# Linear attention ahead of an expert layer: query features projected a second time, transposed, with the exponent's shift added by one-hot products

## The chip, the core and the metric

One core of one Trainium2 chip. TensorE (PE, with its weight loads PEld), VectorE (DVE), ScalarE (ACT), GpSimd (POOL) and the DMA queue that SyncE issues (SP). The metric is the device time of one execution in microseconds; less is better.

## What is computed

Attention with random features (4 batches, 8 heads, 576 positions, head size 64, 128 features), and then a dense mixture of 8 experts on the 2304 tokens of 512 that it gives. In the reference's words:

```python
def phi(x):
    proj = np.einsum('bhsd,md->bhsm', x, omega)
    sq = np.sum(x * x, axis=-1, keepdims=True) / 2.0
    h = proj - sq
    h = h - np.max(h, axis=-1, keepdims=True)
    return np.exp(h) / np.sqrt(m)
q_p, k_p = (phi(q_s), phi(k_s))
kv = np.einsum('bhsm,bhsd->bhmd', k_p, v)
z = np.sum(k_p, axis=2)
num = np.einsum('bhsm,bhmd->bhsd', q_p, kv)
den = np.einsum('bhsm,bhm->bhs', q_p, z)[..., None] + 1e-06
...
for e in range(E):
    h = np.maximum(x @ w1[e], 0.0)
    ye = h @ w2[e]
    out += P[:, e:e + 1] * ye
```

`x` is num / den. `P` comes from gate logits `x @ w_gate` by eight rounds of row and column scaling. All is fp32.

## The kernel before, in words

**Attention.** The work is cut into 36 jobs, 18 for keys and 18 for queries; a job is 128 rows of eight heads (four tiles of 128 by 128, two heads in each). `jobs` lists them: five key jobs, then key and query jobs in turn, then six query jobs alone. `tick` (L847) writes the program of one step: projections, maxima and shifts of the job now, transposes of the next, feature transposes of a query job one step old, numerators and quotients of one two steps old. In the trace's names: `tp` are transposes of raw rows (L374), copied to `th` (L377, L379); `pp` are projections (L389), 8 matmuls, in two row groups of 64; DVE takes maxima (L399), sums the shift (L404) and adds it to one half (L406), ACT takes exps, the other half's with the shift as bias (L415, L419). For keys the features are multiplied by the values (`kv`, L426). For queries they are transposed on TensorE (`qp`, L485), copied by ACT to `qt` (L492), and multiplied by the keys' sums (`np`, L509); DVE divides (L524 to L528), and the tokens are transposed again (`xp`, L544) and copied to `xf` (L550). All matmuls of this stage share six PSUM banks in turn. `squares` (L343) is done by ACT, and its sum by five halvings on POOL (L353).

**Between.** Tokens stand in three chunks of 768. `token_operands` (L101) makes of a chunk seven operands, each cast to a high part on ACT (L119, L123) with the low part beside it, and stores them to DRAM; the sums among them are on POOL, for the last chunk on DVE (L115). `first_splits` and `split` do the same for weights (L272, L276, L246, L247).

**Experts.** Each matrix product is taken as a 2 by 2 of blocks with seven products in place of eight (`ORDER`, L91), and each of these as three matmuls of high and low parts (`first`, L623: `hx`, `hz`; `second`, L737: `x`, `z`, `w`). The first unit starts with the last chunk, whose operands are not reloaded: their matmuls follow their casts.

**What sets the order.** The attention's instructions are pinned: each engine runs them in the order in which `tick` writes them, by dependencies that a loop adds behind `tick`'s calls. After that a scheduler orders the instructions. Loads are issued on SP in the order in which the program names them.

```python
    jobs += k_of(0) + [kr(0)]
    jobs += mix(k_of(1), q_of(0))
    jobs += mix(k_of(2) + [kr(1)], q_of(1))
    jobs += mix(k_of(3), q_of(2))
    jobs += q_of(3) + [qr(0), qr(1)]
```

Of the kernel before, what the change touches and what calls it, by code (L numbers as in the profile page):

```python
# [9 lines left out]
F32 = mybir.dt.float32  # L10
# [12 lines left out]
def moe_attention_kernel(  # L23
# [51 lines left out]
    ps_cm = tc.tile_pool(name="ps", bufs=6, space=bass.MemoryType.PSUM)  # L75
# [4 lines left out]
    def bank(name):  # L80
        return ps[0].tile([P, 512], F32, tag="b", name=name)
# [11 lines left out]
    pinned = []  # L93

# [6 lines left out]
    def token_operands(c, x):  # L101
# [6 lines left out]
        gate_steps = logits(c, x)  # L108
        if last:
            next(gate_steps)  # L110
# [11 lines left out]
        def low(i, o, t):  # L122
            nc.vector.tensor_tensor(t[:, 1], o, raw(t[:, 0]), op=ALU.subtract)  # L123
            xdram[c, i] = xd.tile([P, 2, 2, HL], F32, name=f"xd{c}_{i}")
            nc.sync.dma_start(out=xdram[c, i], in_=raw(t))

        if last:
            for i in ORDER:
                n = len(traced)
# [5 lines left out]
                pinned.extend(traced[n:])  # L135
                xop[0, c, i] = t
                first(0, c, i, 0)
                first(0, c, i, 1)
# [5 lines left out]
        if c == 0:  # L144
            at = {i: {3: q(1, 1), 7: q(0, 1), 2: q(1, 0)}.get(i, q(0, 0)) for i in ORDER}
            plan = "|c1 |c3 l1.s5|c2 l3|c5 l2.s7| l5.s6|c7 |c6 l7| l6.s4| |c4 | l4|"
        else:
            at = {1: q(0, 0), 3: q(1, 1), 2: q(1, 0)}
            for n, i in enumerate((5, 6, 7, 4)):
                at[i] = vts[n].rearrange("p h c -> p (h c)")[:, : 2 * HL].rearrange("p (k t) -> p k t", k=2)  # L150
            plan = "|s5.c1.c3 s7.l1|c2 l3.s6|c5 l2.s4|c7 l5|c6 l7|c4 l6.l4|"
        tiles = {}
        for n, step in enumerate(plan.split()):
            for part in step.split("|"):
                for what in part.split(".") if part else ():
# [3 lines left out]
                    elif what[0] == "c":  # L159
                        tiles[i] = cast(i, at[i])  # L160
                    else:
                        low(i, at[i], tiles.pop(i))
                yield
            next(gate_steps, None)


    def logits(c, x):
# [4 lines left out]
        for h in range(2):  # L172
            lp = bank("lp")
# [8 lines left out]
        yield  # L182
        for h, lg in enumerate(lgs):
            gp = bank("gp")
# [24 lines left out]

    def split(u, w, i):  # L210
# [8 lines left out]
        if w == 1:  # L219
# [10 lines left out]
            o = {1: q(0, 0), 7: q(0, 1), 2: q(1, 0), 4: q(1, 1)}[i] if i not in (5, 6, 3) else tmp[u]  # L230
        else:
# [15 lines left out]
        (nc.vector if u > 0 or (w == 2 and i in (1, 6, 7, 4)) else nc.gpsimd).tensor_tensor(lo, o, raw(hi), op=ALU.subtract)  # L247
# [3 lines left out]
    def first_splits():  # L251
# [10 lines left out]
        for step in "|s5.c1 | l1|c2 |c5 l2| l5.s6.s7| |c4 |c6 l4|c7 l6.s3| l7| |c3 | l3|".split():  # L262
            for part in step.split("|"):
                for what in part.split(".") if part else ():
# [9 lines left out]
                    else:  # L274
                        hi, lo = wt[0, 1, i]
                        nc.vector.tensor_tensor(lo, at[i], raw(hi), op=ALU.subtract)  # L276
                yield


    sc_cm = tc.tile_pool(name="sc", bufs=1, reuse_waits="tile")  # L280
# [9 lines left out]
    om_ps = bank("om_ps")  # L290
    nc.tensor.transpose(om_ps[:, :P], oms.rearrange("p a d -> p (a d)"), ident)
    omt = sc.tile([P, M], F32, name="omt")
    nc.scalar.copy(omt, om_ps[:, :M])

# [16 lines left out]
    def load(which, key):  # L311
# [3 lines left out]
        if key[0] == "r":  # L315
# [5 lines left out]
            else:  # L321
                t = rw.tile([P, H, 1, D], F32, tag=f"{which}r", bufs=2 if which == "q" else 1, name=f"{which}r")
# [11 lines left out]
        else:  # L334
            t = rw.tile([P, H, 2, D], F32, tag=which, bufs=4, name=which)
# [7 lines left out]
    def squares(which, key):  # L343
# [10 lines left out]
        nc.gpsimd.tensor_tensor(o[..., :1], s[..., :1], s[..., 1:2], op=ALU.add)  # L354
        nc.gpsimd.tensor_scalar_mul(o[..., 2], o[..., 0], -1.0)
        sqt[which, key] = o

# [9 lines left out]
    def transposes(jb):  # L367

        which, key, hh = jb[:3]
        tin = rawt[which, key].rearrange("p h j d -> p (h j d)")  # L370
        tp = bank("tp")
        for i in range(4):
            o = (4 * hh + i) * P
            nc.tensor.transpose(tp[:, i * P : (i + 1) * P], tin[:, o : o + P], ident)  # L374
        th = sc.tile([P, 4, P], F32, tag="th", bufs=2, name="th")
        if which == "k":
# [632 lines left out]
```

## Time and profile before

| | us |
|---|---|
| median of 3 runs (lowest to highest) | 1613.35 (1613.24 to 1614.67) |
| profiled execution, its own time | 1611.28 |
| span of its profile | 1609.4 |
| PE busy in the span | 1574.7 |
| DVE busy | 1388.4 |
| ACT busy | 774.8 |
| POOL busy | 298.1 |

The span runs from the first instruction of the profiled execution to its last; the execution's own time is 1.9 longer and is what is compared. Busy times are per engine and overlap. Matmuls are pipelined: a row's printed time holds the last one's way through the array, and what a group takes from the engine is read from its start to the start of the next.

### The profile page before, as it was taken

What the parts mean: (1) busy time and instruction counts of PE and PEld (TensorE: products, weight loads), DVE (VectorE), ACT (ScalarE), POOL (GpSimd) and SP (SyncE); (2) the same over time, 40 slices, a digit from 0 to 9 for tenths busy, and PEclk for the clock granted to TensorE, in tenths of its full rate; (3) what the DMA queues carried; (4) which work ended last, traced back from release to release, by engine and by line L of the source; (5) the groups of instructions that cost most, each with busy time, mean ns of one, the idle gap of its engine ahead of it and who ended that gap; (6) DMA issues with size and microseconds to landing.
All of it is one profiled execution on the core that took longest, in us unless ns stands there. A gap on an engine that the chain in (4) does not pass through costs nothing.

```text
span 1609.4 us, 31434 instructions
## 1 busy us (share of the span) xinstructions
PE 1574.7 (98%) x12318; PEld 1543.1 (96%) x12318; DVE 1388.4 (86%) x2721; ACT 774.8 (48%) x1396; POOL 298.1 (19%) x304
## 2 busy tenths in 40 slices
PE   7998899999999999999999999999999999999998
PEld 6877899999999999999999999999999999999997
DVE  5998798999888987989898988889898889889777
ACT  7987565444344444434354444444443444444333
POOL 6664321101021111101021111112010111110003
PEclk9999999999999999999999999999999999999999
DMA  8646865666665665656656665746565566655552
GB/s 205 153 146 240 305 229 203 212 209 208 220 217 192 233 211 171 224 197 215 206 206 213 211 220 181 253 170 223 203 208 210 211 216 212 212 189 198 193 197 79
DMA packets 105314, 329.79 MB, mean 205 GB/s; under 512 B 14800, under 2 KB 43984, under 8 KB 105168
## 3 DMA queue, kind: packets, MB, share of 16 engines
q1 hardware_dynamic: 105168, 327.79, 60.2%
q8 instruction: 98, 1.61, 0.4%
q14 instruction: 48, 0.39, 0.1%
HBM read 306.53 MB, written 21.23 MB: 204 GB/s over the span
## 4 chain that ended last, share of the span: by engine, by line
PE 86%; DVE 10%; ACT 2%; POOL 1%; issue 1%; DMA 0%; SPq 0%; DVEq 0%; ACTq 0%
PE hx L650 24%; PE x L751 23%; PE hz L650 18%; PE z L751 12%; PE w L751 6%; DVE sm L687 2%; DVE out L777 2%; PE pp L389 1%; DVE bl L687 1%; DVE sqs L399 1%; DVE wl L247 1%; POOL sq L353 1%; DVE sl L726 1%; PE tp L374 1%; DVE xs L123 1%
## 5 line engine op out<-in xcount | busy, mean ns | idle before, releaser
L650 PE MATMUL hx<-xs,wh 128*128 128x384 f32 x1536 | 372.2, 336 | 2.7 <-ACT out L767 1.2
L777 DVE SCALAR_TENSOR_TENSOR out<-x,prob,out 128x256 f32<-128x256 f32 x497 | 234.2, 477 | 59.5 <-PE x L751 57.8
L650 PE MATMUL hz<-xs,wh 128*128 128x384 f32 x1152 | 281.7, 337 | 0.0
L650 PEld LDWEIGHTS hx<-xs,wh 128*128 128x128 f32 x1536 | 268.6, 188 | 4.3 <-ACT xs L119 2.0
L216 POOL TENSOR_TENSOR st<-st 128x512 f32<-128x512 f32 x79 | 126.3, 1598 | 702.6 <-DVE wl L247 698.1
L650 PEld LDWEIGHTS hz<-xs,wh 128*128 128x128 f32 x1152 | 203.2, 189 | 0.7 <-ACT xs L119 0.4
L650 PE MATMUL hx<-xs,wl 128*128 128x384 f32 x768 | 198.7, 335 | 0.0
L729 ACT ACTIVATE bh<-hr 128x512 fp32r<-128x512 f32 x144 | 91.2, 633 | 211.6 <-PE x L751 206.9
L777 DVE SCALAR_TENSOR_TENSOR out<-z,prob,out 128x256 f32<-128x256 f32 x252 | 120.3, 478 | 56.5 <-PE z L751 55.9
L725 ACT CAST sh<-sm 128x512 fp32r<-128x512 f32 x144 | 89.6, 622 | 152.7 <-PE z L751 106.1
L246 ACT CAST wh<-st 128x512 fp32r<-128x512 f32 x172 | 102.9, 620 | 104.6 <-PE hx L650 43.9
L650 PE MATMUL hz<-xs,wl 128*128 128x384 f32 x576 | 151.7, 336 | 0.0
L687 DVE SCALAR_TENSOR_TENSOR sm<-hr,sm 128x256 f32<-128x256 f32 x288 | 137.1, 476 | 2.6
L650 PEld LDWEIGHTS hx<-xs,wl 128*128 128x128 f32 x768 | 138.4, 188 | 0.0
L247 DVE TENSOR_TENSOR wl<-st,wh 128x512 fp32r<-128x512 f32 x169 | 121.8, 730 | 12.0 <-ACT wh L246 11.5
L687 DVE SCALAR_TENSOR_TENSOR bl<-hr,bh 128x512 fp32r<-128x512 f32 x144 | 119.5, 830 | 0.1
L751 PE MATMUL x<-wh,sh 128*128 128x256 f32 x576 | 116.9, 283 | 2.6 <-DVE out L777 1.6
L751 PE MATMUL x<-wl,sh 128*128 128x256 f32 x576 | 118.2, 282 | 0.7 <-DVE wl L247 0.7
L751 PE MATMUL x<-wh,sl 128*128 128x256 f32 x576 | 117.2, 282 | 0.0
L751 PE MATMUL z<-wl,sh 128*128 128x256 f32 x576 | 117.2, 281 | 0.0
L751 PE MATMUL z<-wh,sl 128*128 128x256 f32 x576 | 115.3, 282 | 1.7 <-DVE sl L709 1.7
L751 PE MATMUL z<-wh,sh 128*128 128x256 f32 x576 | 116.6, 281 | 0.2 <-DVE out L777 0.2
(161 smaller groups left out, 3410.5 us busy)
## 6 DMA issues: line engine op xcount, KB each, us to landing
xs<-xd SPq DMA_DIRECT2D x329, 768.0 KB, 4.4
st<-in_moe_w_dram SPq DMA_DIRECT2D x64, 512.0 KB, 5.1
xd<-xs SPq DMA_DIRECT2D x21, 768.0 KB, 4.3
k<-in_k_dram SPq DMA_DIRECT2D x8, 512.0 KB, 7.1
v<-in_v_dram SPq DMA_DIRECT2D x8, 512.0 KB, 6.5
q<-in_q_dram SPq DMA_DIRECT2D x8, 512.0 KB, 7.5
out_dram<-out SPq DMA_DIRECT2D x32, 128.0 KB, 1.9
kr<-in_k_dram SPq DMA_DIRECT2D x4, 128.0 KB, 6.6
```

The costliest lines, as they stand in the source:

```text
L123: nc.vector.tensor_tensor(t[:, 1], o, raw(t[:, 0]), op=ALU.subtract)
L216: nc.gpsimd.tensor_tensor(o, a, b, op=op)
L246: nc.scalar.copy(hi, o)
L247: (nc.vector if u > 0 or (w == 2 and i in (1, 6, 7, 4)) else nc.gpsimd).tensor_tensor(lo, o, raw(hi), op=ALU.subtract)
L353: nc.gpsimd.tensor_tensor(s[..., :w], s[..., :w], s[..., w : 2 * w], op=ALU.add)
L374: nc.tensor.transpose(tp[:, i * P : (i + 1) * P], tin[:, o : o + P], ident)
L650: nc.tensor.matmul(pb, lhsT=a[:, k, g * P : (g + 1) * P], rhs=x[:, b, k, :], start=i in (1, 5, 2) and j == 0, stop=j == len(prods) - 1, sk ...
L687: nc.vector.scalar_tensor_tensor(o, in0=a, scalar=0.0, in1=b, op0=ALU.max, op1=op)
L725: nc.scalar.copy(sh, sm)
L729: nc.scalar.activation(bh, a[:, 1:], AF.Relu)
L751: nc.tensor.matmul(pb, lhsT=ops[s][i][a][:, f], rhs=wt[u, 2, i][b][:, f], start=bool(start) and j == 0, stop=j == len(prods) - 1, skip_gro ...
L777: nc.vector.scalar_tensor_tensor(o, in0=pb, scalar=p, in1=o, op0=ALU.mult, op1=ALU.add)
```

## The change

What it does, part by part:

- **Query features.** The projection of a query job is kept for the maxima alone. Its shift (three numbers of a row summed, twice, into a small tile `cx`) is turned by two matmuls against the identity (`turned_shifts`, `cp`), cast by ACT to a high part and reduced by DVE to a low part beside it (`shift_copy`, `ct`). `features` projects a second time with the operands exchanged, 512 columns a matmul, so that features come out transposed, and adds the shift by eight one-hot products (`pick`, fp32r) into the same banks. ACT takes two exps of 512 columns from PSUM to `qt`. Transposes, copies, bias exps and the add of the old way are gone for queries.
- **Half transposes.** `turn` transposes 64 rows at a time, into two banks; raw rows of a key and a query job share two banks and are copied by ACT.
- **Banks and order.** Six banks are now three pairs, `bk`, `bt`, `bq`; `period` takes the place of `tick` and writes a key and a query job together. One query job (`qr(0)`) moves into the paired part, so 13 pairs and five query jobs alone remain. Tokens are numbered in the order in which the query jobs give them.
- **Squares.** POOL adds twice (the first key job's and the last query job's not at all), and DVE reduces the rest.
- **Token and weight parts.** Low parts of chunks 0 and 1 and of the first unit's first weights move from DVE to POOL. The first unit's second weights have their sums made by POOL during the attention's end, and all their low parts on DVE.
- **First unit.** Its chunks are taken as 1, 2, 0. Chunk 1's operands are used where they are cast; `first` of chunk 1 and of four of seven operands of chunk 2 are left to the scheduler, ahead of the second products.

```diff
-    def bank(name):
-        return ps[0].tile([P, 512], F32, tag="b", name=name)
+    def bank(name, tag=None):
...
+        return ps[0].tile([P, 512], F32, tag=tag, name=name)
...
-            nc.vector.tensor_tensor(t[:, 1], o, raw(t[:, 0]), op=ALU.subtract)
+            (nc.vector if last else nc.gpsimd).tensor_tensor(t[:, 1], o, raw(t[:, 0]), op=ALU.subtract)
...
-        w = D
-        while w > 2:
-            w //= 2
-            nc.gpsimd.tensor_tensor(s[..., :w], s[..., :w], s[..., w : 2 * w], op=ALU.add)
...
+            for w in (D // 2, D // 4) if n < D else ():
+                nc.gpsimd.tensor_tensor(s[..., :w], s[..., :w], s[..., w : 2 * w], op=ALU.add)
...
+            nc.vector.tensor_reduce(o[..., 0], s[..., :n], axis=AX.X, op=ALU.add)
...
+    def turn(tiles, name, tag):
+
+        banks = [bank(name, tag) for _ in range(2)]
+        for i, a in enumerate(tiles):
+            for h in range(2):
+                r = slice(h * 64, (h + 1) * 64)
+                nc.tensor.transpose(banks[h][:, i * 64 : (i + 1) * 64], a[r], ident[r, r])
+        return [bk[:, : 64 * len(tiles)] for bk in banks]
...
+    def turned_shifts(jb):
+
+        cx = cxq.pop(jb)
+        cp = bank("cp", "bt")[:, :P]
+        for g in range(2):
+            nc.tensor.matmul(cp[g * 64 : (g + 1) * 64], lhsT=cx[:, g], rhs=ident, start=True, stop=True)
+        cps[jb] = cp
...
+    def features(jb):
+
+        th, ct = ths.pop(jb), cts.pop(jb)
+        fp = [bank("fp", "bt") for _ in range(2)]
+        for g in range(2):
+            r = slice(g * D, (g + 1) * D)
+            nc.tensor.matmul(
+                fp[g], lhsT=omt[r], rhs=th[r].rearrange("p i s -> p (i s)"), start=True, stop=False,
+                skip_group_check=True,
+            )
+        for i in range(4):
+            for g in range(2):
+                r = slice(g * D, (g + 1) * D)
+                nc.tensor.matmul(
+                    fp[g][:, i * P : (i + 1) * P], lhsT=pick[r, i], rhs=ct[r], start=False, stop=i == 3,
+                    skip_group_check=True,
+                )
+        fps[jb] = fp
+
+    def query_exps(jb):
+
+        qts[jb] = [sc.tile([P, 4, P], F32, tag="ex", bufs=6, name="qt") for _ in range(2)]
+        for t, fp in zip(qts[jb], fps.pop(jb)):
+            nc.scalar.activation(t.rearrange("p i s -> p (i s)"), fp, AF.Exp)
...
-        return [NCH - 1] + list(range(NCH - 1)) if u == 0 else list(range(NCH))
+        return list(range(1, NCH)) + [0] if u == 0 else list(range(NCH))
...
+    pairs = list(zip(k_of(0) + [kr(0)], none))
+    pairs += zip(k_of(1), q_of(0))
+    pairs += zip(k_of(2) + [kr(1)], q_of(1) + [qr(0)])
+    pairs += zip(k_of(3), q_of(2))
+    pairs += [(None, jb) for jb in q_of(3) + [qr(1)]]
```

How PE's order moves in the paired part, one key and one query job before (all names as above):

```order
L389 MATMUL pp<-omt,th 128x128 x8
L374 MATMUL tp<-ident,q 128x128 x4
L485 MATMUL qp<-ident,ex 128x128 x8
L389 MATMUL pp<-omt,th 128x128 x8
L374 MATMUL tp<-ident,k 128x128 x4
L509 MATMUL np<-kvs,qt 64x65 x16
L426 MATMUL kv<-v_96,ex 64x65 x16
```

And now (`fp` is the transposed projection at L500 and the one-hot products at L507, `cp` the turned shift):

```order
L457 MATMUL pp<-omt,th 128x128 x8
L432 MATMUL xp<-ident,xt 128x64 x8
L500 MATMUL fp<-th,omt 128x512 x2
L507 MATMUL fp<-ct,pick 128x128 x8
L457 MATMUL pp<-omt,th 128x128 x8
L432 MATMUL tp<-ident,k 128x64 x8
L432 MATMUL tp<-ident,q 128x64 x8
L612 MATMUL np<-kvs,qt 64x65 x16
L546 MATMUL kv<-v_107,ex 64x65 x16
L482 MATMUL cp<-ident,cx_103 64x128 x2
```

The transposes of both raw jobs stand together, all between the key projections and the numerators uses 64 rows of the array, and `qp` is gone.

ACT in the same place, before:

```order
L492 COPY qt<-qp 128x512 x2
L419 ACTIVATE ex<-pp,cn 128x128 x4
L415 ACTIVATE ex<-ex 128x512
L349 ACTIVATE sq<-q 128x1024
L377 COPY th<-tp 128x512
L419 ACTIVATE ex<-pp,cn 128x128 x4
L272 CAST wh<-st 128x512
L415 ACTIVATE ex<-ex 128x512
```

And now (`ct` is the cast of the shift, `qt<-fp` the query's exps):

```order
L489 CAST ct<-cp 128x128
L309 CAST wh<-t 128x512
L656 COPY xf<-xp 128x4x64 x2
L517 ACTIVATE qt<-fp 128x512 x2
L539 ACTIVATE ex<-pp,cn 128x128 x4
L535 ACTIVATE ex<-ex 128x512
L979 COPY th<-tp 128x8x64 x2
L398 ACTIVATE sq<-qr 128x512
```

The query's exps come first, behind a cast of weights and the token copies, then the key's, and the copies of raw transposes behind both.

PE at the attention's end, before (`lp`, `gp` belong to the gate, `hx` is the first expert matmul):

```order
L485 MATMUL qp<-ident,ex 128x128 x8
L509 MATMUL np<-kvs,qt 64x65 x16
L485 MATMUL qp<-ident,ex 128x128 x8
L544 MATMUL xp<-ident,xt 128x128 x8
L509 MATMUL np<-kvs,qt 64x65 x16
L544 MATMUL xp<-ident,xt 128x128 x4
L509 MATMUL np<-kvs,qt 64x65 x16
L544 MATMUL xp<-ident,xt 128x128 x4
L175 MATMUL lp<-xf,wgs 32x384 x8
L650 MATMUL hx<-xs,wh 128x384 x2
```

And now:

```order
L482 MATMUL cp<-ident,cx_103 64x128 x2
L432 MATMUL xp<-ident,xt 128x64 x8
L500 MATMUL fp<-th,omt 128x512 x2
L507 MATMUL fp<-ct,pick 128x128 x8
L612 MATMUL np<-kvs,qt 64x65 x32
L190 MATMUL lp<-xf,wgs 32x384 x4
L432 MATMUL xp<-ident,xt 128x64 x24
L756 MATMUL hx<-xs,wh 128x384 x2
```

The last two numerators stand together, then three tokens' transposes; the first `hx` is now chunk 1's.

## Rows read from the trace of the kernel before

**Rows 1.** Busy time in four stretches; columns: stretch, length, engines with counts, clock, DMA.

```profile
24.55:117.55 93.00, 88.83 (x1514) 77.32 (x1514) 83.32 (x186) 84.61 (x205) 63.28 (x109) 1.00 0.57 153
117.55:154.87 37.32, 33.38 (x470) 26.37 (x466) 33.39 (x82) 31.16 (x72) 18.42 (x22) 1.00 0.53 195
154.87:186.25 31.38, 25.32 (x133) 23.34 (x134) 25.54 (x37) 16.98 (x30) 10.68 (x7) 0.95 0.88 342
186.25:240.00 53.75, 53.75 (x380) 53.48 (x379) 48.94 (x108) 32.28 (x67) 11.47 (x9) 1.00 0.70 239
```

**Rows 2.** Timeline of PE, one pair of jobs; columns: start us, us, what, idle before.

```profile
66.23 1.16 PE L389 MATMUL pp<-omt,th 64*128 64x128 f32 x16
67.32 0.65 PE L374 MATMUL tp<-ident,q 128*128 128x128 f32 x4
67.81 1.04 PE L485 MATMUL qp<-ident,ex 128*128 128x128 f32 x8
68.82 1.16 PE L389 MATMUL pp<-omt,th 64*128 64x128 f32 x16
69.91 0.66 PE L374 MATMUL tp<-ident,k 128*128 128x128 f32 x4
70.50 1.15 PE L509 MATMUL np<-kvs,qt 128*64 128x65 f32 x32
71.48 1.13 PE L426 MATMUL kv<-v,ex 128*64 128x65 f32 x32
72.88 1.16 PE L389 MATMUL pp<-omt,th 64*128 64x128 f32 x16 [0.27 <-ACT th L377]
```

**Rows 3.** Timeline of weight loads (PEld) around a matmul of 8 columns.

```profile
205.31 0.30 PEld L588 LDWEIGHTS cp<-cs,ones 128*128 128x128 f32 x2
205.53 0.30 PEld L650 LDWEIGHTS hx<-xs,wh 128*128 128x128 f32 x2
```

**Rows 4.** Timeline of ACT in the paired stage.

```profile
75.69 1.12 ACT L492 COPY qt<-qp 128x512 f32<-128x512 f32 x2
76.63 1.23 ACT L419 ACTIVATE ex<-pp,cn 128x128 f32<-128x128 f32 x4
77.64 0.73 ACT L272 CAST wh<-t 128x512 fp32r<-128x512 f32 x1
...
78.62 0.75 ACT L415 ACTIVATE ex<-ex 128x512 f32<-128x512 f32 x1
79.16 0.70 ACT L377 COPY th<-tp 128x512 f32<-128x512 f32 x1
79.62 1.27 ACT L419 ACTIVATE ex<-pp,cn 128x128 f32<-128x128 f32 x4
```

**Rows 5.** Timeline of DVE in the paired stage.

```profile
68.08 0.68 DVE L379 COPY th<-tp 128x512 f32<-128x512 f32 x1
...
69.47 0.18 DVE L404 TENSOR_REDUCE cn<-sqs 128x8 f32<-128x24 f32 x1
69.68 0.69 DVE L406 TENSOR_TENSOR ex<-pp,cn 128x512 f32<-128x512 f32 x1
70.29 1.28 DVE L399 TENSOR_REDUCE sqs<-pp 128x4 f32<-128x512 f32 x2
```

**Rows 6.** Timeline of PE: last projection, a wait in the tail, a later wait.

```profile
140.73 1.16 PE L389 MATMUL pp<-omt,th 64*128 64x128 f32 x16
...
149.61 0.63 PE L544 MATMUL xp<-ident,xt 128*128 128x128 f32 x4 [1.38 <-DVE xt L528]
...
179.27 0.50 PE L751 MATMUL z<-wh,sl 128*128 128x256 f32 x2 [1.68 <-DVE sl L709]
```

**Rows 7.** Chain that ended last, 120 to 200 us; columns: start us, us, what.

```profile
132.74 1.43 PE lp L175 x16
...
137.80 0.77 PE gp L186 x6
...
188.07 2.11 PE hx L650 x12
```

More of the change, by code (lines that the diff above doesn't have):

```diff
@@ L845, in go_on, with products, turned_raw @@
                 extra.remove(it)
-    def tick(j):
-        def job(n, which=None):
-            return jobs[n] if 0 <= n < len(jobs) and which in (None, jobs[n][0]) else None
-        now, nxt = job(j), job(j + 1)
+    def products(jb):
+        it = keys_by_values(jb)
+        next(it)
+        leftover.append(it)
+    def turned_raw(jbs, tag):
+        for n, (to, tp) in enumerate(transposes(jbs, tag)):
+            if n == 0 and jbs[0][0] == "k" and len(jbs) == 1:
+                nc.vector.tensor_copy(to, tp)
+            else:
+                nc.scalar.copy(to, tp)
@@ L853, in tick, with pair_at, ahead, period @@
+    def pair_at(i):
+        return pairs[i] if 0 <= i < len(pairs) else (None, None)
+    def ahead(i):
+        return max([-1] + [jobs.index(jb) for p in pairs[: i + 1] for jb in p if jb])
+    def period(i):
+        k, qn = pair_at(i)
+        done = pair_at(i - 1)[1]
+        nxt = [jb for jb in pair_at(i + 1) if jb]
+        add_squares()
         while closing:
             kv_close(*closing.pop(0))
-        if now:
-            projections(now)
-            maxima(now, 0)
-        ensure_squares(j)
@@ new lines, in period @@
+        if k:
+            go_on()
+            projections(k)
+            maxima(k, 0)
+            maxima(k, 1)
+            if nxt and not qn:
+                turned_raw(nxt, "bt")
+            shifts(k)
+        if i < 0:
+            turned_raw(nxt, "bt")
+        if k or not qn:
+            sum_squares()
+        if i < 0:
+            ensure_squares(i)
+            sum_squares()
+        alone = qn and not k
+        tail = i >= len(pairs)
+        if alone:
+            projections(qn)
@@ L878, in tick @@
         leftover.clear()
-        if job(j - 2, "q"):
-            numerators(job(j - 2))
-        if job(j - 1, "k"):
-            it = keys_by_values(job(j - 1))
-            next(it)
-            leftover.append(it)
-        if job(j - 2, "q"):
-            quotients(job(j - 2))
-        go_on()
+        while waiting:
+            products(waiting.pop())
+        if done:
+            query_exps(done)
+        if k:
+            exps(k, 1)
+            exps(k, 0)
+        if qn:
+            if not alone:
+                projections(qn)
+            maxima(qn, 0)
+            maxima(qn, 1)
+            query_shifts(qn)
+            if alone:
+                sum_squares()
@@ new lines, in period @@
+        if nxt and qn and k:
+            turned_raw(nxt, "bt")
+        while untaken:
+            untaken.pop(0)()
+        if k:
+            ensure_squares(i)
+        else:
+            go_on()
+        if done:
+            behind.append(done)
+        while len(behind) > (1 if alone else 0):
+            numerators(behind[0], "bq" if tail and len(behind) == 1 else "bk")
+            quotients(behind.pop(0))
+        if nxt and alone:
+            turned_raw(nxt, "bq")
+            ensure_squares(i)
@@ L900, in moe_attention_kernel @@
             extra.append(it)
[L901 removed]
+        if i == 16:
             stage(0, 2)
[L903 removed]
+        period(i)
         ensure_loads(i + 1)
[L905 to L913 removed]
+    for i in range(len(pairs), len(pairs) + 4):
+        period(i)
+    while untaken:
+        untaken.pop(0)()
+    ended.append(1)
     while extra or at_last:
@@ L980, in moe_attention_kernel @@
         ops.pop(s)
+    for ins in traced[since:until]:
+        if ins.engine == mybir.EngineType.Pool:
+            tc.add_manual_dep(ins, before[ins.engine], in_order, reason="order of the weights' sums")
+            before[ins.engine] = ins.name
 _INS = ["q", "k", "v", "omega", "moe_w_gate", "moe_w1", "moe_w2"]
```

357 lines of the change are left out of this document (220 added, 137 removed).

## The prediction

> **What bounds the kernel now.** I read first the busy time by stage [rows 1]. From 186 us on, PE is busy in every microsecond (53.75 of 53.75): the expert stage is bound by TensorE, and the change leaves its matmuls as they are (same counts, same shapes). What can move is what lies ahead: 24.55 to 117.55 (13 key jobs, 12 query jobs), 117.55 to 154.87 (six query jobs alone, then the last tokens), and 154.87 to 186.25, where the expert matmuls have begun but PE is busy only 25.32 of 31.38.
>
> Second, one pair of jobs in PE's order of time [rows 2]: from the projection at 66.23 to the next key-side one at 72.88, back to back but for a wait of 0.27. In this stage ACT is busy 84.61 and DVE 83.32 of 93.00 as well [rows 1], so three engines are near their limit at once, and relief of one alone buys little.
>
> Third, the same stage on ACT and DVE [rows 4, 5]: what one instruction takes from the engine is the distance from its start to the next one's, less than its printed time. ACT: two `qt` copies 0.94, four biased exps 1.01, one 512-wide exp 0.54, a copy of `th` 0.46. DVE: two maxima, a copy or a 512-wide add about 0.60 each.
>
> **Prices on PE.** A weight load of 128 columns follows the last after 0.11 us even where the matmul between has 8 columns (two in 0.22) [rows 3]. The transposes step 0.12 each (4 in 0.49) and so stand at that load, not at their moving columns [rows 2]. The projection has 8 matmuls, two records each, in two row groups that run side by side: first to last start is 1.16 less one record's 0.28, so 0.89 with its own step, 0.11 for a pair. A change of array form (64 rows, 128 by 128, 64 columns) costs 0.1 to 0.2: transposes take 0.49 before transposes and 0.59 before the numerators, projections 1.09 before transposes [rows 2].
>
> **The change, a pair of jobs on PE.** Removed: 8 transposes of query features (1.01) and three of five form changes (0.45), since half transposes, both projections, the transposed projection and the one-hot products all use 64 rows. Added: the transposed projection has as many columns per row group as the first one (512, two records), 0.89; eight one-hot products with 128-column weights, four pairs, 0.44; the shift's transpose, two matmuls of 128 columns, 0.25. The half transposes load the same 128 columns as a whole one, so 4 pairs take 0.44 as the whole ones did; their lower bound is the pace of products with 64-column weights (32 records in 0.98, 0.06 a pair [rows 2]). I take the load's pace, since [rows 3] is the nearest case of small moving tiles. Sum of the period: three projections 2.67, key, query, token and one-hot pairs 1.76, numerators and key-value 1.96, shift 0.25, two form changes 0.30: 6.94. Before, the same list is 6.33 by [rows 2], plus one token transpose 0.53, plus the wait 0.29: 7.15. So PE, the engine that binds, gets nothing from the new query path.
>
> The Trainium skill speaks here with two voices. "TensorEngine Tiling (Array Packing)", Overview, gives up to 2x for contractions of 64 rows or less; by it the half transposes would take half. "TensorE: Matmul & The Clock Gate", LDWEIGHTS, says that a load's time goes with its columns and not with its rows; the trace's 0.11 agrees. By the first the sum would be lower by about 0.6 a period, which is the first rival below.
>
> **ACT and DVE.** ACT loses per pair two copies (0.94), four biased exps (1.01), and gains half a `th` copy's worth twice over (0.46) and a 128-wide cast (0.3 at most): 1.2 less. DVE loses a copy, a 512-wide add and the small sum (1.4) and gains two small sums, two 32-row subtracts (0.2 each by the small sum [rows 5]) and a reduce of squares (0.35): 0.3 less, and the low parts of tokens and first weights go to POOL, which was busy 63 of 93 [rows 1]. Both now have room; that room costs nothing and gives nothing while PE binds.
>
> **One wait is added.** The new order's banks `bt` hold the transposes, the shift and the features in turn. PE puts the next half transposes 0.89 (one projection) behind the last one-hot product; ACT must first empty both feature banks: 0.25 to notice, two exps of 0.54, so 1.33. PE waits 0.45. Bounds: nothing, if the first bank's exp starts early, to 1.3, if ACT is still at its cast and token copies. With it the period is 7.4. Queued behind that wait are the numerators and key-value products.
>
> **Sum.** Paired part: 13 periods of 7.4 are 96.2, less features, numerators and token transposes that the first periods lack (3.6), plus three half gates (a whole one 1.43) and one set of gate transposes 0.77 [rows 7]: 95.5, from 24.55 to 120.05, one query job further than the old 117.55. The first five key jobs I leave at their time; DVE's reduce takes over POOL's five adds there (bounds: 1.5 gained, 0.5 lost). Then five query jobs alone: PE needs 0.89 + 0.44 + 0.89 + 0.44 + 0.98 + 0.44 + 0.25 + 0.45 of form changes, 4.78, and the next projection waits some 0.4 for ACT's copies of the half transposes: 5.2 each against 4.64 (23.2 for five [rows 1, 6]). Last projection: 120.05 + 4 x 5.2 = 140.85, where it was at 140.73 [rows 6]. From there the old order needs 14.1 to the first expert matmul, with a wait of 1.38 for quotients, and another like it, since the jobs go through one by one [rows 6]. The new tail issues the last two numerators together and three tokens in three bank pairs: 4.2 to the shift's transpose, 3.6 to the end of both numerators less overlap, 0.8 of quotients not covered by the gate, 1.7 of token transposes: 10.3. Expert matmuls start at 151.15, **3.7 earlier**.
>
> Now the third stage. Before, the expert matmuls of the last tokens start as these tokens are cut into parts, and PE waits 6.06 in 31.38; the granted clock is 0.95 in the mean, after waits of which the longest, 1.68, ends at 179.27, so a tenth of the stage runs at the lower level (1.2 for 2.4 GHz), 1.6 lost [rows 1, 6]: 7.6 in all. The new order puts chunk 1 first, whose parts are ready, so its seven tiles of 12 matmuls, 2.11 each [rows 7], cover the casts of chunk 2 with 14.8 us. DVE then has a run of seven weight parts (0.6 each) and left operands behind the last token part, for which I leave 3.0 of waits; 0.7 more gate work falls into the stage. **3.9 gained.** POOL's work is no longer in DVE's way there.
>
> Together 7.6 from 1611.28, the profiled execution's own time, gives 1603.7; that execution stands 2.1 below the median of 1613.35, which gives 1605.7 on the scale of the median. I say **1605**.
>
> **Rivals.** *Half transposes at the pace of 64-column weights* (0.06 a pair for 0.11): 12 pairs a period fewer 0.05, 0.6, times 13, plus 0.4 in five jobs alone: 10 less, 1595. For it: moving columns are halved. Against: [rows 3]. *Given back*: the head start of chunk 1 is worth nothing because DVE is the later one until chunk 2's steps. In [rows 1] it was busy 25.54 of 31.38 while PE waited, and it keeps all low parts of chunk 2 and now all seven weight parts: 3.9 + 2 more, 1611; no change, with 1610 to 1616. *The `bt` banks are the bound* (slower): transposes, shift and features hand the same two banks round, each emptied by ACT; if ACT's exps come one copy and one cast later than I place them, the wait is 1.3, 0.85 more in 13 periods and 0.5 in five: 13.5 lost, 1618.5. It decides from a period of 7.95, where the whole gain is gone. For it: ACT is busy nine tenths of the stage and its order (below the diff) puts cast and token copies ahead of the exps. Against: those copies end before the one-hot products do, and ACT has 1.2 less to do.
>
> **The numbers.** A difference under 0.2% (3.2 us, 1610.1 to 1616.6) cannot be told from none by such runs. My forecast 0.50 (1598 to 1610), half transposes faster 0.15 (1588 to 1598), given back 0.17, banks 0.18. So faster 0.65, same 0.17, slower 0.18. The range 1593 to 1618 takes in the unchanged cases, half of the fast one and of the slow one; some 0.17 lies outside.
>
> **What would show it.** In the changed profile: starts of the first query-side projections 7.2 to 7.6 apart; half transposes 8 in about 0.5 (0.25 would be the first rival); the one-hot products 8 in 0.45 and the 512-wide projection 0.9; PE's waits before half transposes on ACT's exps of 0.2 to 0.6 (over 1 would be the third); last query projection near 141, first expert matmul near 151; PE waits of about 3 in the 30 us after it, at a DVE low part, and a granted clock of 1.00 there. I am wrong if the paired part ends before 113 or after 127, or if expert matmuls start on time and PE then waits over 6.

## The result: 1630.3 us, 1.0% slower, and the profile after

The changed kernel takes 1630.26 us (median of 3 runs, 1629.26 to 1631.19) against 1613.35; the ratio is 1.0102, 95% interval 1.0079 to 1.0125. Forecast were 1605, so the prediction is wrong by 25 us and on the wrong side. The profiled run is the median one: 1630.26 us, span 1628.3, which is 18.9 more than the span of before.

The busy time by stage, cut at the same events as in [rows 1] (first paired key projection, first projection of the jobs alone, first expert matmul); columns as there:

```profile
27.93:125.77 97.84, 94.37 (x1789) 80.64 (x1786) 75.05 (x210) 76.30 (x184) 58.00 (x61) 1.00 0.54 143
125.77:162.19 36.42, 32.36 (x484) 25.38 (x482) 21.57 (x71) 18.33 (x45) 22.83 (x17) 0.95 0.32 130
162.19:194.00 31.81, 30.25 (x177) 28.45 (x175) 19.25 (x28) 19.57 (x33) 7.34 (x4) 1.00 0.67 257
194.00:250.00 56.00, 48.87 (x315) 46.53 (x314) 52.75 (x103) 30.42 (x66) 15.59 (x10) 0.94 0.63 220
```

ACT and DVE were relieved (76.30 and 75.05 us in the paired part for 84.61 and 83.32), and the part got no shorter: PE is busy there for 94.37 of 97.84. The surprise is the last row: where the kernel before had PE busy without a gap, DVE is full (52.75 of 56) and PE stands 7.1 us, at a granted clock of 0.94.

One pair of jobs on PE, timeline, to be held against [rows 2]:

```profile
61.81 0.39 PE L482 MATMUL cp<-ident,cx 128*64 128x128 f32 x4
62.13 1.32 PE L457 MATMUL pp<-omt,th 64*128 64x128 f32 x15
...
66.24 0.46 PE L432 MATMUL tp<-ident,k 64*128 64x64 f32 x7 [0.19 <-ACT qt L517]
66.47 0.47 PE L432 MATMUL tp<-ident,q 64*128 64x64 f32 x8
66.88 1.15 PE L612 MATMUL np<-kvs,qt 128*64 128x65 f32 x32
67.86 1.10 PE L546 MATMUL kv<-v,ex 128*64 128x65 f32 x32
68.79 0.39 PE L482 MATMUL cp<-ident,cx 128*64 128x128 f32 x4
```

The period is 6.98, the wait at the feature banks 0.19. The start of the execution and the attention's tail (from the last projection to the first expert matmul) on PE:

```profile
22.35 0.44 PE L432 MATMUL tp<-ident,k 64*128 64x64 f32 x8
22.59 0.45 PE L432 MATMUL tp<-ident,q 64*128 64x64 f32 x8
23.07 1.15 PE L546 MATMUL kv<-v,ex 128*64 128x65 f32 x32
26.85 1.15 PE L546 MATMUL kv<-vr,ex 64*64 64x65 f32 x32 [2.63 <-POOL sq L408]
27.93 1.16 PE L457 MATMUL pp<-omt,th 64*128 64x128 f32 x16
...
147.58 1.37 PE L457 MATMUL pp<-omt,th 64*128 64x128 f32 x15
...
151.53 0.39 PE L482 MATMUL cp<-ident,cx 128*64 128x128 f32 x4
152.75 0.76 PE L432 MATMUL xp<-ident,xt 64*128 64x64 f32 x8 [0.83 <-DVE xt L631]
...
155.45 3.60 PE L612 MATMUL np<-kvs,qt 128*64 128x65 f32 x64
160.11 0.85 PE L190 MATMUL lp<-xf,wgs 128*32 128x384 f32 x8 [1.06 <-DVE xt L631]
160.90 1.37 PE L432 MATMUL xp<-ident,xt 64*128 64x64 f32 x24
162.19 0.62 PE L756 MATMUL hx<-xs,wh 128*128 128x384 f32 x2
```

Eight half transposes start 0.24 apart from the next eight: 0.06 a pair, half of what was forecast. The first expert matmul comes at 162.19, where it was at 154.87. From it to the span's end are 1466.1 us, before 1454.5. So 7.3 of the 18.9 us are lost ahead of the expert stage, 11.6 in it.

The stage's longest waits (who waited <- for whom: us in total, times, longest), 162.1 to 250:

```profile
PE z L866 <- DVE out L884: 2.1, 1, 2.1
PE x L866 <- DVE sl L841: 1.6, 2, 1.1
PE hz L756 <- DMA xs<-xd: 1.1, 1, 1.1
PE w L866 <- DVE bl L802: 1.0, 1, 1.0
PE z L866 <- ACT sh L823: 0.8, 1, 0.8
PE hz L756 <- ACT xs L123: 0.7, 1, 0.7
```

### The profile page after: what moved, and what is told of

Read it like the earlier page. It is cut to its first block, busy times and chain, and to the rows that moved or that the text cites. A ratio compares the mean times of both kernels' runs of the same rounds, so it can differ in the third digit from the quotient of the medians.

```text
span 1628.3 us, 32099 instructions
## 1 busy us (share of the span) xinstructions
PE 1588.1 (98%) x12678; PEld 1553.6 (95%) x12678; DVE 1371.0 (84%) x2754; ACT 760.3 (47%) x1363; POOL 299.4 (18%) x240
## 4 chain that ended last, share of the span: by engine, by line
PE 87%; DVE 8%; issue 2%; ACT 2%; DMA 1%; POOL 0%; SPq 0%; DVEq 0%; ACTq 0%; POOLq 0%
PE hx L756 23%; PE x L866 22%; PE hz L756 18%; PE z L866 11%; PE w L866 5%; DVE out L892 2%; PE pp L457 2%; DVE sm L802 1%; PE np L612 1%; DMA xs<-xd 1%; PE fp L500 1%; DVE bl L802 1%; PE kv L546 1%; DVE wl L284 1%; DVE sl L841 1%
## 5 line engine op out<-in xcount | busy, mean ns | idle before, releaser
L866 PE MATMUL z<-wh,sh 128*128 128x256 f32 x576 | 118.3, 283 | 3.0 <-DVE out L884 2.1
L802 DVE SCALAR_TENSOR_TENSOR bl<-hr,bh 128x512 fp32r<-128x512 f32 x144 | 118.3, 821 | 1.4 <-ACT bh L844 1.4
L866 PE MATMUL z<-wl,sh 128*128 128x256 f32 x576 | 117.3, 282 | 0.0
L814 ACT ACTIVATE ah<-hr 128x256 fp32r<-128x256 f32 x144 | 60.4, 420 | 120.9 <-PE x L866 119.2
```

Source lines behind the costliest of these rows:

```text
L802: nc.vector.scalar_tensor_tensor(o, in0=a, scalar=0.0, in1=b, op0=ALU.max, op1=op)
L814: nc.scalar.activation(ah, a11, AF.Relu)
L866: nc.tensor.matmul(pb, lhsT=ops[s][i][a][:, f], rhs=wt[u, 2, i][b][:, f], start=bool(start) and j == 0, stop=j == len(prods) - 1, skip_gro ...
```

## The experiments

Profiled spans are about 2 us below the runs' times. A span is compared with a span, a median with a median; the kernel before was run beside each group (medians 1612.3 to 1613.5). Brackets behind a time hold its ratio to the kernel before and the 95% interval of that ratio.

### Where the second layer's left operands lie

From step to step of the expert stage the changed kernel fell further behind, long after its last odd wait. Taken over all neighbouring records less than 250 ns apart from 300 to 1500 us, second-layer records started 119.2 ns apart before and 120.1 after (this distance is called the pitch below). The diff had moved the tiles `sh`, `sl`, `bh`, `bl` from the pool `hp` on SBUF's right side to `op`. **`place`** puts them into a pool of their own on the right:

```
+    hq = ctx.enter_context(tc.tile_pool(name="hq", bufs=1, side="right", reuse_waits="tile"))
...
-        sh = op_.tile([P, 2, 2, P], F32R, tag="sh", bufs=1, name="sh")
+        sh = hq.tile([P, 2, 2, P], F32R, tag="sh", bufs=1, name="sh")
```

(and so for the other five). Expected:

> Only the SBUF place of the left operands of the second layer (sh, sl, bh, bl, 12 KB a partition) differs from the change: a pool of their own at 114656 to 126944 on the right side, beside where the kernel before keeps them (145376 to 157664), and not at 75712 to 88000, right behind the weight parts that the same matmuls read as moving data (18368 to 75712). Between 300 and 1500 us the second layer's matmul records start 119.2 ns apart in the kernel before and 120.1 in the change, while those whose left operand is ah or al, which lie on the right side in both, are at 117 in both. Theory P, the place sets the pitch: it falls to about 119.2, 6048 records by 0.9 ns, so 5 us less than the change (about 1625). Theory Q, it comes from the order or the banks of the expert stage: 0 to 1 us less.

**`before_op`** does the reverse to the kernel before (`hp_[0].tile` becomes `op_.tile` in these six lines):

> The kernel before with the same tiles at the change's addresses (75712 to 88000), nothing of the attention changed; the first left operands are issued behind the first weight split, since the pool opens later. Theory P, the place sets the pitch: 120.1 ns for 119.2, 5 us more than the kernel before (about 1618). Theory Q, order or banks: 0 to 1 us more. Its start also shows how far the start of a run of the same attention differs from one run to another.

Measured: `place` 1627.04 us (1.0085, 1.0068 to 1.0101), pitch 119.29; `before_op` 1616.99 against 1612.69 (1.0025, 1.0015 to 1.0034), pitch 120.04. Theory P holds both ways, more clearly by the pitch than by the time: `place` gained 3.2 us and not 5, in a run whose profile lost clock at the start (0.50 from 26 to 36), and `before_op` lost 4.3. In each of these pairs PE runs the expert stage's matmuls in the same order, so the order is not what differs. It can be read in the timeline, from the first `sh` record of a run to the record behind its last; the changed kernel, twenty records in 2.40 us:

```profile
1003.93 0.40 PE L866 MATMUL z<-wh,sh 128*128 128x256 f32 x2
...
1006.09 0.40 PE L866 MATMUL w<-wh,bh 128*128 128x256 f32 x2
1006.33 0.40 PE L866 MATMUL w<-wl,bh 128*128 128x256 f32 x2
```

and the run `place`, the same twenty in 2.36:

```profile
1004.80 0.39 PE L866 MATMUL z<-wh,sh 128*128 128x256 f32 x2
...
1006.92 0.40 PE L866 MATMUL w<-wh,bh 128*128 128x256 f32 x2
1007.16 0.40 PE L866 MATMUL w<-wl,bh 128*128 128x256 f32 x2
```

A third run moved them below the weight parts instead of above (`left_operands_a(0)` and `_b(0)` ahead of the splits):

> The change with the left operands (sh, sl, bh, bl) at 18368 to 30656, below the weight parts that the same matmuls read (30656 to 88000), where the change has them above (75712). If what counts is that they lie in the same part of SBUF as those weight parts (theory P1), the pitch of the second layer's records stays at 120.1 ns; if it is the address in the change itself (P2), it falls to 119.2 as on the right side.

The pitch stays at 120.09 in its one run: theory P1. By left operand, neighbours of one kind under 200 ns apart: `sl` 118.2 ns before and 118.3 in `place`, 119.6 in the change, `before_op` and `place_low`; `ah` and `al`, never moved, 118.1 each before, 118.3 and 117.5 in the change. So two places on the left give the longer pitch and two on the right the shorter. Whether it is the nearness to the weight parts that the same matmuls read, or the left part itself, is not shown, since the weight parts were never moved; what in the SBUF makes it so wasn't tried. 6048 records by 0.87 ns are **5.3 us** of the 18.9, an estimate from the pitch.

### The stall at the start

> Two orders at the start of the change: the products of the first key job of the rest rows wait for the next key job's projection (they were issued right behind their own exponents, and PE stood 2.63 us before them at 26.85), and DVE's reduce of the squares in the first five jobs comes behind the next job's maxima (it waited for POOL's adds and held the maxima from 22.55 to 23.57). Theory S, this order costs the start 3.4 us: projection of the first pair about 2.5 us earlier against the first job, 1.5 to 2.5 us less time than the change. Theory L, the loads set the start: no change, and the wait moves to a load.

The edit let the first rest rows' products wait for the next projection, and held back DVE's reduce:

```
-            if qn or k[1][0] == "r":
+            if qn:
                 products(k)
```

Measured 1630.53 (1.0106, 1.0091 to 1.0121): no gain, and neither theory. The projection did come earlier, at 25.71, but PE then stood three times (0.89, 0.45, 1.30), on DVE and ACT and on no load: 2.64 in sum, as much as the one wait before. The granted clock fell to 0.50 from about 30 to 36. That drop is the second price of the stall: it shows in seven of the ten profiled runs that keep the change's order here, as in the run `gate_late` (told below), where the same matmuls take 2.08 for 1.16:

```profile
27.27 2.00 PE L546 MATMUL kv<-vr,ex 64*64 64x65 f32 x32 [2.63 <-POOL sq L408]
29.20 2.08 PE L457 MATMUL pp<-omt,th 64*128 64x128 f32 x16
```

**`start2`** also issues both projections of the first pair around these products, each in the other's banks:

> The start once more: as the run before on the start, and both projections of the first pair are issued around the products of the first rest rows' keys, in other banks, so that PE has work while exponents and the copy of the first sums are on the way. In the change PE stands 2.63 us at 24, and in six of the eight changed kernels profiled so far the granted clock then falls to 0.50 for 4 to 8 us (28 to 36), 3 to 4 us lost. Theory S, the stall brings the clock down: with stalls under 1 us the clock stays at 1.00, first shift transpose at 31 to 33 (33.4 to 38.2 so far), 3 to 5 us less than the change. Theory E, the clock falls there for what came before: it falls again, 1 to 2 us less.

Measured 1627.75 (1.0089, 1.0074 to 1.0104), 2.5 less. The waits are 0.75 and 0.45, the clock stays at 1.00, and the first expert matmul is at 160.60:

```profile
26.30 1.16 PE L469 MATMUL pp<-omt,th 64*128 64x128 f32 x16 [0.75 <-ACT th L991]
27.91 1.15 PE L558 MATMUL kv<-vr,ex 64*64 64x65 f32 x32 [0.45 <-POOL sqs L414]
28.99 1.16 PE L469 MATMUL pp<-omt,th 64*128 64x128 f32 x16
```

The first shift transpose is at 33.1, as in the changed profile, which happened to keep its clock, and 2 to 5 us ahead of the runs that lost it. The clock bears theory S out, here and in the five other runs with this start; the 2.5 us lie below its 3 to 5.

### Half transposes taken back

```
...
-                nc.tensor.transpose(banks[h][:, i * 64 : (i + 1) * 64], a[r], ident[r, r])
+            nc.tensor.transpose(banks[i // n][:, i % n * P : (i % n + 1) * P], a, ident)
```

> Every half transpose (64 rows, two row groups) goes back to a whole one of 128 rows, in the same banks and with as many copies of the same size as the change has; all else is the change's. In the changed trace 8 half pairs take 0.48 for two jobs and 0.24 for a token tile; whole ones stepped 0.12 each in the kernel before, so 0.97 and 0.49. Theory A, PE sets the paired periods: each grows by 0.5 to 0.75, in 13 periods and five jobs alone 8 to 10 us, so the time is 8 to 10 us above the change's. Theory B, ACT's or DVE's order sets them (PE could wait less instead): 0 to 3 us above the change's.

Measured 1634.96 (1.0141, 1.0125 to 1.0156), 4.7 above the change; from the first to the last shift transpose 123.1 us for 118.1, so 5.0 by the trace. The period that was 6.98 is 7.60:

```profile
65.29 0.39 PE L482 MATMUL cp<-ident,cx 128*64 128x128 f32 x4
...
69.95 0.66 PE L431 MATMUL tp<-ident,k 128*128 128x128 f32 x4
70.44 0.60 PE L431 MATMUL tp<-ident,q 128*128 128x128 f32 x4
70.97 1.15 PE L612 MATMUL np<-kvs,qt 128*64 128x65 f32 x32
...
72.89 0.39 PE L482 MATMUL cp<-ident,cx 128*64 128x128 f32 x4
```

Between the theories, and by the time nearer to B. This period grows by 0.62, though the wait of 0.19 goes, and runs without a gap, as A has it. But of the twelve paired periods that can be measured so, three grow by 0.58 to 0.62 and four not at all (0.01 to 0.18 shorter). So PE's work sets a part of the periods, and in the rest something else hides it. Of this change, the half transposes are a part that earns something.

### Why the expert stage began worse

Four runs looked for causes. **`gate_late`** moves the last tokens' gate behind their parts (`next(gate_steps)` out of the loop); there it reads token rows that the sums have overwritten, so its gate values differ. **`gl_pf`** also puts the first part ahead of the waiting adds, with the same gate. **`gate_early`** has the gate in full: its second half in bank `bk` as the last token is copied, the rest behind the parts. **`steps343`** changes `(2, 2, 2)` to `(3, 4, 3)`.

> The gate of the last tokens (second half of its products, its transposes, its reduce) is issued behind all seven token parts of the last chunk and not between the first and the third. In the changed trace ACT's cast of the second part stands behind the copy of those products (174.12), and DVE's subtraction for the third behind the reduce (178.44). Theory A, the late parts are what makes DVE's queue overflow from 194 to 246: parts end about 5 us earlier (last low part at 186 for 191.4), and waits and clock loss of the stage (11.5 us in the change) fall by 4 to 6 us. Theory B, too little first-layer work is left for PE in the first three steps, whose DVE work is longer than PE's whatever comes before: 0 to 1.5 us less.

> As the run with the late gate, and the first token part of the last chunk (cast and low part) is issued ahead of the waiting copies and adds of the chunk before it, which held ACT until 169.46 and DVE until 170.34 in the changed trace. Theory A, late parts: parts end 8 to 10 us earlier than in the change (last low part at 181 to 184), and the time falls by 7 to 9 us against the change. Theory B, first three steps short of PE work: 0 to 2 us.

> The last tokens' gate in full: the second half of its products right behind the last token's copies (in a bank that the pieces of the chunk before don't hold), its transposes and reduce behind the seven parts. In the change the gate stood between the first and the third part on ACT and DVE. Theory A, late parts are what fills DVE's queue from 194 to 246: last low part 25 us or less behind the first expert matmul (29.2 in the change), 3 to 5 us less than the change. Theory C, the four token tiles hold the parts (a cast waits for a tile that PE must first have read): last low part moves by 3 us at most and the time by 0 to 3 us.

> One number table: in the first three steps of the expert stage 3, 4 and 3 first-layer pieces are issued (as the kernel before has it) and not 2, 2 and 2; four pieces of the next chunk move ahead by a step or two. Theory B, too little first-layer work for PE in these steps: each piece is 1.04 us of PE work, so 3 to 4 us less. Theory A, DVE's queue is late for what came before: the pieces bring DVE adds of 0.9 each as well, and need loads that land late, so from 1 us more to 1.5 us less.

Measured 1626.85 (1.0085, 1.0068 to 1.0102), 1632.37 (1.0119, 1.0101 to 1.0138), 1632.68 (1.0121, 1.0105 to 1.0136) and 1629.78 (1.0108, 1.0092 to 1.0124). From the first expert matmul to the last low part: 29.2 us in the change, 26.4, 26.0 and 26.6 with the gate moved. So the gate holds the parts by 3 us and no more, as theory C says. Its reason, token tiles that PE's pieces still hold, is seen on ACT for a part alone: in `gl_pf` two casts of the last chunk's parts wait for PE, 0.89 in sum, where ACT also stands 2.05 for POOL's low parts and 2.08 for a sum on DVE:

```profile
174.00 0.84 ACT L123 CAST xs<-hr 128x768 fp32r<-128x768 f32 x1 [0.47 <-PE hz L756]
...
178.11 0.84 ACT L123 CAST xs<-xf 128x768 fp32r<-128x768 f32 x1 [0.42 <-PE hz L756]
```

Against the change the times are 3.4 us less, 2.1 more, 2.4 more and 0.5 less. The three with the gate moved differ by 6 us, and the one with the earliest parts, `gl_pf`, is not the fastest, so theory A's gain is not seen; why `gate_early` is slower than the change stayed open. `steps343` moves nothing: theory B is out.

The chain itself can be seen on ACT and DVE of the changed kernel; first ACT (the gate's copy waits for PE, the cast of a part stands behind it), then DVE:

```profile
173.74 0.48 ACT L195 COPY lg<-lp 128x384 f32<-128x384 f32 x1 [3.44 <-PE lp L190]
174.12 0.84 ACT L123 CAST xs<-hr 128x768 fp32r<-128x768 f32 x1
```

```profile
169.86 0.56 DVE L774 TENSOR_TENSOR hr<-hz,hr 128x384 f32<-128x384 f32 x1 [7.06 <-PE hz L756]
170.34 0.95 DVE L127 TENSOR_TENSOR xs<-xf,xs 128x768 fp32r<-128x768 f32 x1
...
190.46 0.96 DVE L127 TENSOR_TENSOR xs<-xf,xs 128x768 fp32r<-128x768 f32 x1
...
192.44 0.68 DVE L284 TENSOR_TENSOR wl<-st,wh 128x512 fp32r<-128x512 f32 x1
```

DVE has nothing for 7 us while PE works on the pieces of chunk 1, then cuts until 191.4, and only then come eight weight parts (the change splits the fourth one twice) and the left operands.

**`sink_late`** takes DVE work away: `if k in (1, 4) and s >= NP`.

> The normalisation of the gate (eight rounds over rows and columns, about 15 us of DVE, needed only by the fifth of sixteen units) begins nine steps later, at the second unit; nothing else differs from the change. Theory A, DVE's queue from 194 to 246 is what PE waits for there: with 10 to 15 us less in that queue the waits of 208 to 250 (4.2 us) go and part of those before it, 4 to 6 us less than the change. Theory D, PE waits for the chain of each step (left operands, casts, DVE, PE) and not for DVE's load: 0 to 1 us less.

Measured 1639.14 (1.0157, 1.0142 to 1.0172): 9 more, which no theory had. The waits up to 250 stay (8.0 us of PE idle for 8.7), which speaks against theory A but does not settle it: DVE's busy time from the first expert matmul to 250 fell by 2.3 us alone, and not by 10 to 15. The loss stands where PE had been full, in waits and in the clock. It is not the moved work's for certain: behind this edit PE also runs the expert matmuls in another order than in the change, from 198 us on. Busy time up to 250 and from 350 to 600, first this run, then the change:

```profile
160.90:250.00 89.10, 81.10 (x519) 77.62 (x517) 69.75 (x113) 52.28 (x100) 23.63 (x15) 0.98 0.69 247
...
350.00:600.00 250.00, 244.04 (x1677) 240.79 (x1676) 219.93 (x448) 104.13 (x173) 33.51 (x21) 0.98 0.57 195
```

```profile
162.19:250.00 87.81, 79.12 (x490) 74.98 (x488) 72.00 (x130) 49.99 (x97) 22.93 (x14) 0.96 0.64 233
...
350.00:600.00 250.00, 247.62 (x1737) 245.81 (x1736) 215.97 (x415) 108.63 (x180) 36.33 (x24) 1.00 0.60 205
```

**`old_order`** undoes the whole start of the expert stage:

```
-        return list(range(1, NCH)) + [0] if u == 0 else list(range(NCH))
+        return [NCH - 1] + list(range(NCH - 1)) if u == 0 else list(range(NCH))
...
-                if i in ORDER[:4]:
-                    first(0, c, i, 0)
-                    first(0, c, i, 1)
+                first(0, c, i, 0)
+                first(0, c, i, 1)
```

> The change's attention with the expert stage begun as the kernel before begins it: the last tokens' chunk first, all its 14 first-layer pieces as its parts are cut, chunk 1 cut and stored without pieces ahead, 3, 4 and 3 pieces in the first steps, every weight part made once (the change makes the fourth twice); left operands at the change's addresses. Theory H, the pieces issued ahead are what costs: they hold the four token tiles and the fixed order of ACT and DVE, so that the last chunk is cut from 169 to 191 and not from 162 on, the weights and left operands of the second layer come behind that, and by then PE's pieces are used up. Then the stage from the first expert matmul to the end falls from 1466 to 1460 (1454.5 in the kernel before, and 5 for the place of the left operands): 4 to 6 us less than the change. Theory D', the waits after 194 belong to the steps' own chains, whatever comes first: 0 to 1 us less.

Measured 1630.17 (1.0111, 1.0094 to 1.0128), as the change, its clock at 0.53 and 0.61 from 28 to 36. Its first expert matmul waits for the cut (165.80), and its stage is 1462.4 us, 3.7 less than the change's. What the stage gains by the old order, its later start takes back; the next pair of runs shows it without the clock's drop at the start.

### Together

> The right-side place of the left operands and the new start together, all else the change's. If both hold and add: 3 to 5 us and 2.5 us less than the change, 1622 to 1625.

> All three: place, start, and the expert stage begun as in the kernel before. If theory H holds: 4 to 6 us below the run with place and start, 1617 to 1620; what is then left to 1613 is the attention itself, whose first expert matmul comes 5 us later than in the kernel before. Theory D': 1622 to 1625.

`place_start` takes 1622.16 (1.0055, 1.0040 to 1.0070), `best3` (old order as well) 1623.29 (1.0065, 1.0050 to 1.0080). Place and start add: 8.1 us less than the change, and against `start2` alone the place is worth 5.6, as the pitch says. Neither run lost clock at the start, so they compare the two orders best. The first expert matmul comes 9.4 us behind the last shift transpose in `place_start` and 12.8 in `best3`, and the stage then takes 1461.0 and 1456.8: together 1470.4 and 1469.6, while the medians differ by 1.1 the other way. **The order in which the expert stage begins is worth about 1 us at most**, and theory H falls as a loss, as the forecast's gain does. What `place_start` still lacks to the kernel before is, by the spans, 4.7 us ahead of the first expert matmul and 6.5 behind it; no run removed these.

Two runs joined the late normalisation to place and start, the second with three low parts on POOL:

> The place of the left operands (right side), the start of the run before and the late normalisation, together. If the three are independent and theories P, S and A hold: 5 + 4 + 5 = 14 us less than the change, 1616. If A falls: 1621. If S falls as well: 1624.

> As the run with the three, and three of the seven low parts of the first second-layer weights go to POOL (as the kernel before has four of seven there in part), 1.8 us less for DVE from 192 to 199. Theory A: 1 to 2 us less than the run with the three. Theory D: the same, or 1 more, since POOL takes 1.3 us for each where DVE takes 0.6 and products wait for them.

1633.23 (1.0120, 1.0103 to 1.0137) and 1632.18 (1.0116, 1.0101 to 1.0131): they carry the late normalisation's loss, and the 1.1 between them lies within their intervals. The last run moves the next job's half transposes ahead of the numerators in the jobs alone:

> The run with place and start, and in the five query jobs alone the next job's half transposes stand ahead of the numerators and not behind them, so that ACT copies them while PE is at the numerators. In the change the next projection waits 0.41 to 0.59 for these copies in two of five jobs and the shift's transpose 0.45 once. If the wait goes and none takes its place: 1 to 2 us less (1620 to 1621). If the half transposes then wait for DVE's maxima to free their banks: no change.

The waits shrank (first to last shift transpose 117.3 us for 118.1), and the time is 1627.06 (1.0090, 1.0073 to 1.0107), 5 more than `place_start`. The scheduler, which orders the expert matmuls, dealt them anew there, from 208 us on, and the stage is 6.8 us longer. That the order is what costs is argued and not shown, and why it would be worse stayed open. No version here beats the kernel before.

## Why the prediction was wrong

By its own steps, profiled run against profiled run: forecast 1603.7 against 1630.26, 26.5 us, of which 11.0 stand at the first expert matmul (151.15 against 162.19) and 15.5 behind it.

| step | forecast | measured | off |
|---|---|---|---|
| five key jobs at their time | 24.55 | 27.93 | +3.4 |
| paired part | 95.5 | 97.84 | +2.3 |
| four jobs alone | 20.8 | 21.81 | +1.0 |
| tail | 10.3 | 14.61 | +4.3 |
| waits, clock and gate of the third stage | 3.9 gained | 4.7 lost | +8.6 |
| pitch of the second layer | unchanged | 5.3 lost | +5.3 |

That leaves 1.6 unaccounted for.

**The period came out below its forecast, by errors that partly cancel.** Half transposes take 0.24 for eight, so the first rival had the pace right and [rows 3] misled: the pace of a 128-row load was carried over to 64 rows. Rows and moving columns were halved together, and no run separates the two. The Trainium skill, "TensorEngine Tiling (Array Packing)", Overview, has the halving as a gain of up to 2x; the trace's 0.06 for 0.12 agrees with it, and not with the price by columns alone that the forecast found in the Trainium skill, "TensorE: Matmul & The Clock Gate", LDWEIGHTS. Against that, a projection takes 1.00 (forecast 0.89) and the shift's transpose 0.32 (0.25). Single periods of 6.93 to 7.25 are below the 7.4 forecast, the wait 0.19 below 0.45, and the `bt` rival never came near its 1.3. The sum still missed by 2.3: six other periods take 7.8 to 9.1. The gate work in four of them was in the sum; waits of 0.41 and 0.43 for token and gate copies, and a second set of products of 1.08 in the period of the second rest rows' keys, were not. Two slips did not move the time: [rows 2] give the old list 6.38 and not 6.33, and ACT was relieved by 0.64 a pair (84.61 and 76.30 over 13) and not by 1.2, since the query's second 512-wide exp, 0.54, was left out.

**The start was left out.** "The first five key jobs I leave at their time" looked at DVE's reduce only. But the new order issues the rest rows' products behind their own exponents, and DVE's reduce waits for POOL ahead of the maxima: 2.63 of wait, out of the bounds of 0.5, and usually a clock drop with it. Undoing these two orders alone (`start`) left 2.64 of waits; only with other work for PE beside the chain (`start2`) did they fall to 1.20.

**The tail** was priced by engines, not by the chain; this is read from the trace, and no run changed it. Between the last shift transpose and the last numerators stand ACT's cast, DVE's subtractions, the features and ACT's exps, 3.9 us (151.53 to 155.45), while PE has only one token and the features to do. The double numerators then took 3.60, partly at the low clock; `start2` has 2.09 there and a tail of 13.3, so about 3 of the 4.3 us remain without the clock's drop.

**The third stage.** The head start of chunk 1 was to gain 3.9. Idle time is 8.7 from 162.19 to 250, and 200 to 208 at a clock of 0.59 costs 2.8 more, against 6.1 and 1.6 before; with 0.8 of gate work that moved into the stage it is worse by 4.7. That the head start is given back was the second rival, and `place_start` beside `best3` shows it: 3.4 us ahead, 4.2 longer. Its mechanism (DVE is the later one) is not shown. PE's longest waits do name DVE's results, but `sink_late`, with some of DVE's work moved, waits nearly as long. So why PE waits there stays open.

**The place of a tile** was in the diff and in no step: "the change leaves its matmuls as they are (same counts, same shapes)" put it at nothing. With 5.3 us by the pitch, 3.2, 4.3 and 5.6 by three pairs of medians, it is the largest single term that was shown by experiment, and both ways.

Of what was to show the forecast wrong, the paired part ended at 125.77, inside its bounds of 113 and 127. The other sign, expert matmuls on time and PE then waiting over 6 us, was met by half: PE waited 8.7, but the matmuls came 11 us late, which neither sign named.

So the steps that failed are the start (left at its time, 3.4 late), the tail (10.3 forecast, 14.6 measured), the gain of the third stage (3.9 forecast, 4.7 lost) and the tiles' place (no term, 5.3). Place and start are shown by runs; tail and third stage are read from traces.

## What to carry to other kernels

A change to one stage also moves tiles, pools and the order of what follows: look in the diff for tiles that changed their pool, and compare the pitch of the matmuls in the stage that "stays as it is". Relief for engines that don't bind gave nothing here, while a stall of 2 to 3 us in front of a binding TensorE can be paid twice, in the wait and in the clock. A small edit can make a scheduler deal the rest of the program anew: compare the order before a difference is put down to the edit. A head start is worth only what its next user can take: count the buffers and the fixed orders that stand in front of it.

## Not expected of the hardware

- The same matmul records start 119.2 or 120.1 ns apart, by where the left operand's tile lies (three runs moved it; the cause is open).
- Transposes of 64 rows (64 moving columns) in two row groups take 0.06 us a pair, whole ones 0.12.
- After PE's wait of 2.63 us at 24 us (2.32 in `whole`) the granted clock fell to 0.50 (1.2 GHz) for 7 to 10 us in seven of the ten profiled runs that keep that order, and in `start`, with 2.64 in three waits. It stayed at 1.00 in the three others and in all six with the second start, whose waits there are about 0.75 and 0.45.
